# Weights' bound from TensorE products instead of a VectorE reduction, no filling products, and three more units with one exponential

## The chip, the cores and the metric

The kernel runs on one core of a Trainium2 chip. The metric is device microseconds of one execution, taken as the median of several runs. A profiled execution has its own time; its trace covers a span that is a little shorter. The engines are named as the profile names them: PE (TensorE's products) with PEld (its weight loads), DVE (VectorE), ACT (ScalarE), POOL (GpSimd) and SP (SyncE, which issues the DMAs).

## The reference

Linear attention with positive random features is followed by a two-layer network. Batch, heads, sequence and head width are 8, 8, 576 and 64, there are 128 features, and the network has widths 512, 2048 and 512 over 8 x 576 = 4608 tokens.

```python
scale = 1.0 / np.sqrt(np.sqrt(D))
q_s, k_s = (q * scale, k * scale)

def phi(x):
    proj = np.einsum('bhsd,md->bhsm', x, omega)
    sq = np.sum(x * x, axis=-1, keepdims=True) / 2.0
    h = proj - sq
    h = h - np.max(h, axis=-1, keepdims=True)
    return np.exp(h) / np.sqrt(m)
q_p, k_p = (phi(q_s), phi(k_s))
kv = np.einsum('bhsm,bhsd->bhmd', k_p, v)
z = np.sum(k_p, axis=2)
num = np.einsum('bhsm,bhmd->bhsd', q_p, kv)
den = np.einsum('bhsm,bhm->bhs', q_p, z)[..., None] + 1e-06
attn = (num / den).astype(np.float32)
...
h = x @ w_in          # x: attn, heads side by side, 4608 x 512
g = 0.5 * h * (1.0 + erf(h * inv_sqrt2))
return (g @ w_out).astype(np.float32)
```

The two weight matrices come in as 64-bit floats and are brought to 32 bits on the core.

## The kernel before, in words

**Units.** A unit is one batch entry with two heads; there are 32, numbered in order of the batch, so units 0 to 3 are the first batch entry. Units 0 to 7 are "plain": for each, `pair` (L657) and `shared` (L664) make the projections of k and q in 18 tiles of 128 x 128, which lie in five groups in the accumulation memory (PSUM); `top` (L669, DVE) takes the row maxima of a group. Then there are two ways to the exponential. In mode 0, `exp_tiles` (L673, ACT) takes each of the 18 tiles with its own maximum as the bias. In mode 1, `shift_tiles` (L678, DVE) subtracts the maxima group by group, five instructions in all, and `exps` (L682, ACT) then takes all 2304 columns in one instruction. `X['m0']` says how many units are of mode 0. After that come `kv` (L689), a copy of its result (L697, L698), the transposes of q (`q_trans` L727, copied out by `q_copy` L731), the numerator and denominator (`num_plain` L737), the reciprocals (`rcp`, L763 to L766) and the division (`div`, L800). Units 8 to 31 use products of split halves (L902, L924, L1003, L746).

**Weights.** Each matrix comes in eight pieces of 128 partitions x 1024 numbers (1 MB each as 64-bit words), first `w_in` and then `w_out`. `w_load` (L422) brings a piece into one of two buffers `raw`. On it work `w_hi` (L426, ACT; the upper words to a float), `w_rmax` (L438, DVE; the largest absolute upper word of each partition), `w_lo` (L435, ACT; the lower words), `w_shift` (L442, DVE; three bits to the left) and `w_round` (L453, POOL; adds the lower part), which leaves the 32-bit piece in `w32`. When all eight pieces of a matrix have their maximum, `wchain_a` to `wchain_f` (L500, L503, L506, L509, L512, L518 to L521) make one power of two of it for the whole core, the scale. With it `w_high` (L485, ACT) and `w_low` (L489, DVE) split the matrix into a high and a low half of 16 bits.

**Network.** The 4608 tokens are cut into blocks of 128, eleven times 384, and 256. Block 0 is computed in 32 bits straight from `w32` (L1176 first layer, L1187 gelu, L1202 second layer), so it needs no scale. All later blocks use three products of halves for each 32-bit product (L1181 first layer, L1205 to L1207 second layer).

**Order.** A planner goes through all operations with a cost for each, their due times (tables `STARTS`, `UDUE`, `OFF`) and a hand-kept list of operations that come first (`FIRST`). Its result is the fixed order of instructions on each engine; on the chip, each engine takes its instructions in that order and waits where an input is not there. While the planner's clock lies between 5 and `X['wk']` = 100 us and PE has nothing ready, it puts in a `fill` (L381): four products of the identity, whose result nobody reads.

**Accumulation memory.** There are eight banks: two fixed ones (`hb`), three of a ring `at` and three of a ring `acc`. The plain units of the first batch entry may take any of them, the others `at` alone.

Of the kernel before, what the change touches and what calls it, by code (L numbers as in the profile page):

```python
# [11 lines left out]
BF16 = mybir.dt.bfloat16  # L12
# [7 lines left out]
P = 128  # L20
T = 384
# [6 lines left out]
X = dict(fb=793.51, fbp=-272.45, fb0=327.13, fbb=-89.81, fbw=0.0, pm=0.088, tsw=1.28, wmaxp=0, plain=8, kvp=8, eb0=8, ttr=1,  # L28
         pair=0, amax=0, qm=1, xm=0, km=0, prelu=1, vs=1, rm=1, wk=100.0, wk0=5.0, nd=1, sr=0, pmx=0, m0=5)
# [3 lines left out]
STARTS = (526.64, 413.1, 498.14, -519.29, 750.73, 290.96, 409.8, 1471.02, 410.3, 561.38, 1804.53, 1092.9, 2449.47, 1437.07)  # L33
UDUE = (138.05, 1052.37, 451.76, -315.56, -8.29, -412.87, -648.85, -667.31, -702.59, -616.51, 659.91, -322.47, 26.1, 555.78,
# [4 lines left out]
OFF = dict(block_be=26.55, block_high=27.77, block_low=-66.27, block_out=-28.64, block_scales=3.6, block_spread=19.77,  # L39
           bound_b=-1.8, bound_c=-2.45, chain_a=-30.63, chain_b=-10.13, chain_c=-20.24, den=42.52, div=27.82, exp_tiles=19.68,  # L40
           exps=188.48, g_high=-4.72, g_low=-2.69, gelu=-0.61, k_high=-188.65, k_low=1.15, k_shift=6.34, kv=-46.75, kv_a=19.82,
           kv_b=26.2, kv_b2=28.0, kv_c=85.59, kv_d=-177.32, kv_split=-133.22, kvz_plain=-8.08, load_dup=-16.98, load_om=49.87,
           load_two=-48.56, load_v=-10.04, load_vraw=0.87, load_vst=9.94, mm1=-0.7, mm2=6.86, nothing=115.9, num=-9.4,
           num_plain=-14.95, p2=-1.38, pair=14.61, proj=20.5, proj_add=90.32, proj_lo=-1.05, proj_q=-2.91, q_back=-44.1,
           q_blocks=93.79, q_copy=3.3, q_high=-144.85, q_low=-2.94, q_max=87.36, q_max2=100.29, q_max3=-0.43, q_max4=12.08,
           q_max5=4.81, q_max6=-30.09, q_shift=-0.46, q_trans=-45.18, rcp=31.74, shared=-0.95, shift_tiles=7.84,
           split_om=35.99, store=-8.53, store_dma=-54.03, top=-1.35, v_a=53.83, v_b=-6.0, v_max=-0.96, v_scales=80.74,
           w_hi=58.87, w_high=6.68, w_lo=0.74, w_load=-11.85, w_low=3.77, w_rmax=11.16, w_round=-18.28, warm=5.19,
           wchain_a=35.94, wchain_b=91.67, wchain_c=-1.79, wchain_d=18.88, wchain_e=5.29, wchain_f=-87.86, x_high=-1.56,
           x_low=0.31, zeros=71.27)  # L50
FIRST = (1, 3, 0, 2, 6, 7, 8, 40, 4, 5, 42, 110, 76, 144, 41, 142, 10, 9, 151, 157, 44, 13, 43, 11, 14, 15, 47, 74, 16, 45, 17,
# [208 lines left out]
def favor_attention_ffn(ctx: ExitStack, tc: tile.TileContext, qT, kT, v, omT, w_in, w_out, out):  # L260
# [281 lines left out]
    def weights_in(win, i):  # L542
# [19 lines left out]
        if X['rm']:  # L562
            return
# [833 lines left out]
```

## Time and profile before

| what | value |
|---|---|
| median of 3 runs | 976.95 us (976.17 to 978.94) |
| the profiled execution | 975.53 us |
| its span | 973.8 us |
| PE busy | 963.4 us, 6324 instructions |
| DVE busy | 715.4 us, 1948 instructions |
| ACT busy | 730.0 us, 1504 instructions |
| POOL busy | 350.4 us, 560 instructions |

An engine's busy time is the time in which at least one of its instructions is under way. PE's products overlap, so the duration of one (322 ns for L1181) is longer than the time until the next starts; how many products pass in a stretch of the chain of waits gives the pace. Filling products count as busy like all others. Rows of a timeline begin with start and length in us; rows of groups hold busy time, mean ns of one, and what ended the idle time before them.

### The profile page before, as it was taken

How to read it: one execution, taken by the hardware profiler on the slowest of the kernel's cores; microseconds unless marked ns; L12 is line 12 of the kernel's file. 1: busy time of each engine (PE TensorE's matmuls, PEld its weight loads, DVE VectorE, ACT ScalarE, POOL GpSimd, SP SyncE). 2: the span in 40 equal slices, each digit the busy share in tenths (PEclk: the TensorE clock that was granted, in tenths of full speed). 3: DMA queues.
4: the chain of work that ended last, by engine and by line, in shares of the span. 5: the costliest groups of instructions: out<-in, count | busy, mean ns of one | idle time of the engine just before them, and what ended most of it. 6: DMA issues, size and time to landing. Idle time of an engine off the chain costs nothing.

```text
span 973.8 us, 18152 instructions
## 1 busy us (share of the span) xinstructions
PE 963.4 (99%) x6324; PEld 602.3 (62%) x6324; DVE 715.4 (73%) x1948; ACT 730.0 (75%) x1504; POOL 350.4 (36%) x560
## 2 busy tenths in 40 slices
PE   8999999999999999999999999999999999999998
PEld 7777665665566666666565665566656656555576
DVE  5899899977888889878797888777767778621111
ACT  6979897887689879787798878877776986643243
POOL 2444334742166264353255335245216522200000
PEclk9999999999999999999999999999999999999999
DMA  8756123321041041031221132022003200000000
GB/s 305 229 182 227 70 73 134 98 82 55 1 118 61 26 139 47 25 91 45 75 82 49 30 127 66 14 72 61 24 33 86 62 23 12 1 33 1 1 34 22
DMA packets 39083, 70.96 MB, mean 73 GB/s; under 512 B 5712, under 2 KB 14288, under 8 KB 38992
## 3 DMA queue, kind: packets, MB, share of 16 engines
q1 hardware_dynamic: 38992, 69.81, 23.1%
q8 instruction: 50, 0.82, 0.4%
q14 instruction: 41, 0.34, 0.1%
HBM read 60.36 MB, written 9.44 MB: 72 GB/s over the span
## 4 chain that ended last, share of the span: by engine, by line
PE 96%; DVE 2%; DMA 1%; ACT 0%; issue 0%; SPq 0%; ACTq 0%; DVEq 0%
PE hb L1181 37%; PE acc L1205 12%; PE acc L1207 12%; PE acc L1206 12%; PE at L746 4%; PE at L924 3%; PE at L902 3%; PE at L1003 2%; PE hb L381 2%; PE hb L1176 2%; PE acc L1202 1%; PE at L657 1%; PE at L737 1%; PE at L689 1%; PE hb L689 1%; PE at L727 1%
## 5 line engine op out<-in xcount | busy, mean ns | idle before, releaser
L1181 PE MATMUL hb<-xh,wih 128*128 128x384 f16 (+1 forms) x768 | 247.2, 322 | 0.6 <-DVE gl L1197 0.4
L1181 PE MATMUL hb<-xl,wih 128*128 128x384 f16 (+1 forms) x768 | 247.2, 322 | 0.0
L1181 PE MATMUL hb<-xh,wil 128*128 128x384 f16 (+1 forms) x768 | 247.1, 322 | 0.0
L894 POOL TENSOR_TENSOR r<-xt,r 64x256 fp32r<-64x256 f32 (+2 forms) x216 | 171.8, 814 | 202.7 <-ACT r L889 161.3
L1205 PE MATMUL acc<-woh,gh 128*128 128x512 f16 (+1 forms) x560 | 211.4, 377 | 0.0
L1207 PE MATMUL acc<-wol,gh 128*128 128x512 f16 (+1 forms) x560 | 210.5, 376 | 0.0
L1206 PE MATMUL acc<-woh,gl 128*128 128x512 f16 (+1 forms) x560 | 210.5, 376 | 0.0
L1197 DVE SCALAR_TENSOR_TENSOR gl<-hb,bs,gh 128x384 f16<-128x384 f32 (+1 forms) x192 | 115.2, 600 | 126.0 <-ACT gh L1193 124.2
L1181 PEld LDWEIGHTS <-wih 128*128 128x128 f16 x1536 | 147.0, 98 | 95.2 <-issue 1.7
L1189 ACT ACTIVATE hb<-hb,bs 128x384 f32<-128x384 f32 (+1 forms) x192 | 104.5, 545 | 86.8 <-PE hb L1181 84.5
L1193 ACT ACTIVATE gh<-hb,bs 128x384 f16<-128x384 f32 (+1 forms) x192 | 109.2, 569 | 51.5 <-PE acc L1207 35.5
L1181 PEld LDWEIGHTS <-wil 128*128 128x128 f16 x768 | 75.1, 98 | 50.2 <-issue 1.6
L889 ACT CAST r<-xt 128x256 fp32r<-128x256 f32 (+2 forms) x216 | 81.5, 403 | 25.8 <-PE at L902 10.5
L1207 PEld LDWEIGHTS <-gh 128*128 128x128 f16 x576 | 56.4, 98 | 64.5
L1205 PEld LDWEIGHTS <-gh 128*128 128x128 f16 x576 | 56.1, 97 | 47.4 <-issue 0.4
L1206 PEld LDWEIGHTS <-gl 128*128 128x128 f16 x576 | 56.5, 98 | 42.1
L803 DVE TENSOR_TENSOR w<-at,rt 64x128 f32<-64x128 f32 (+6 forms) x168 | 54.7, 325 | 4.3 <-DVE rt L770 0.5
L757 ACT ACTIVATE dt<-at,vsc 64x288 f32<-64x288 f32 x96 | 47.6, 495 | 5.2 <-PE at L746 3.0
L902 PE MATMUL at<-om,r 128*128 128x256 f32 x216 | 50.3, 325 | 0.2
L924 PE MATMUL at<-r,om 128*128 128x288 f32 x192 | 50.4, 351 | 0.0
L906 ACT COPY lo<-at 128x256 f32<-128x256 f32 (+1 forms) x120 | 40.4, 349 | 2.2 <-PE at L902 1.5
L963 DVE TENSOR_TENSOR ql<-qt,qh 128x576 fp32r<-128x576 f32 x48 | 37.3, 782 | 6.1 <-ACT qh L960 6.0
(218 smaller groups left out, 1690.6 us busy)
## 6 DMA issues: line engine op xcount, KB each, us to landing
xt<-in_kT SPq DMA_DIRECT2D x56, 288.0 KB, 3.8
xt<-in_qT SPq DMA_DIRECT2D x56, 288.0 KB, 3.6
out_x<-o SPq DMA_DIRECT2D x35, 256.0 KB, 2.1
raw<-in_w_in SPq DMA_DIRECT2D x16, 512.0 KB, 5.2
raw<-in_w_out SPq DMA_DIRECT2D x16, 512.0 KB, 4.6
w<-in_v SPq DMA_DIRECT2D x6, 1280.0 KB, 6.1
wol<-in_v SPq DMA_DIRECT2D x6, 320.0 KB, 5.9
vt<-in_v SPq DMA_DIRECT2D x2, 320.0 KB, 4.1
```

Of the source, the lines that this page charges most:

```text
L803: nc.vector.tensor_tensor(x[r, c0:c1], ps[r, r0:r1], rt[r, r0:r1], op=ALU.mult)
L889: nc.scalar.copy(G['r', u, x][:, 0:b - a], xf[:, a:b])
L894: nc.gpsimd.tensor_tensor(r, xf[D:, a:b], r, op=ALU.subtract)
L902: nc.tensor.matmul(o[:, t], r[:, t * P:(t + 1) * P], om, start=True, stop=True)
L924: nc.tensor.matmul(G['pp', u, NK + g][:, 0:HS], om[:, i], xr_part(u, NK + g), start=(i == 0), stop=(i == 1))
L1181: nc.tensor.matmul(h[:, 0:t], w, (G['xh', n, j], G['xh', n, j], G['xl', n, j])[k][:, 0:t], start=(i == 0), stop=(i == 3 * NJ - 1))
L1189: nc.scalar.activation(h, h, AF.Gelu, scale=G['bs', n][:, 2:3])
L1193: nc.scalar.activation(G['gh', n, c][:, 0:t], G['h', n, c][:, 0:t], AF.Copy, scale=G['bs', n][:, 3:4])
L1197: nc.vector.scalar_tensor_tensor(G['gl', n, c][:, 0:t], G['h', n, c][:, 0:t], G['bs', n][:, 3:4], G['gh', n, c][:, 0:t], op0=ALU.mult, op1 ...
L1205: nc.tensor.matmul(acc, gh[:, s], woh[:, c, c0:c1], start=(c == 0), stop=False)
L1206: nc.tensor.matmul(acc, gl[:, s], woh[:, c, c0:c1], start=False, stop=False)
L1207: nc.tensor.matmul(acc, gh[:, s], wol[:, c, c0:c1], start=False, stop=(c == NF - 1))
```

## The change

It has three parts, and all the planner's tables are new.

1. `w_rmax` is gone. In its place `w_gram` multiplies, on PE, each of a piece's eight 128 x 128 squares with itself; the operand is the upper 16 bits of each 32-bit number of the finished piece, read as bf16. Four pieces add up in one bank of accumulation memory (`GP = 4`). After the fourth, `w_gmax` (DVE) takes the maximum of the bank's 128 columns. The diagonal holds sums of squares, so its maximum bounds the square of the largest weight; `wchain_e` and `wchain_f` halve the exponent. Since the operand is the finished piece, this stands behind `w_round`, where `w_rmax` stood behind the load.
2. `X['wk']` goes from 100 to 0, so no `fill` is put in. (A flag inside `fill` changes too, without effect since it isn't called.)
3. `X['m0']` goes from 5 to 2: units 2, 3 and 4 take mode 1. `shift_tiles` now writes to the unit's own buffer.

```diff
-X = dict(fb=793.51, fbp=-272.45, ..., vs=1, rm=1, wk=100.0, wk0=5.0, nd=1, sr=0, pmx=0, m0=5)
+X = dict(fb=839.08, fbp=-293.81, ..., vs=1, rm=1, wk=0.0, wk0=5.0, nd=1, sr=0, pmx=0, m0=2, gm=1, rawn=2)
...
-FIRST = (1, 3, 0, 2, 6, 7, 8, 40, 4, 5, 42, 110, 76, 144, 41, 142, 10, 9, 151, 157, 44, 13, 43, 11, 14, 15, 47, 74, 16, 45, 17,
+FIRST = (1, 3, 76, 6, 2, 0, 8, 7, 42, 41, 40, 144, 4, 5, 111, 153, 9, 10, 159, 15, 11, 43, 146, 16, 12, 74, 13, 44, 17, 49, 47,
...
+    def w_gram(pc):
+        o = G['gram', pc.win, pc.i // GP][:, 0:P]
+        for x in range(8):
+            a = pc.b.bitcast(BF16).rearrange("p (x m t) -> p x m t", x=8, t=2)[:, x, :, 1]
+            nc.tensor.matmul(o, a, a, start=(pc.i % GP == 0 and x == 0), stop=(pc.i % GP == GP - 1 and x == 7))
+
+    def w_gmax(win, g):
+        nc.vector.tensor_reduce(wmax[:, win, g:g + 1], G['gram', win, g][:, 0:P], axis=AX.X, op=ALU.max)
...
     def wchain_f(win):
         e, s, r = (wsc[:, win, i:i + 1].bitcast(I32) for i in range(3))
         one = float(1 << 23)
-        if X['rm']:
+        if X['gm']:
+            nc.gpsimd.tensor_scalar(e, e, 0.5, 65 * one, op0=ALU.mult, op1=ALU.add)
+        elif X['rm']:
...
-        if X['rm']:
+        if X['rm'] and not X['gm']:
             op('DVE', 1.23, w_rmax, pc, r=[rk], w=[('wmax', win, i)])
...
+        if X['gm']:
+            g = ('gram', win, i // GP)
+            op('PE', 0.46, w_gram, pc, r=bk, w=[g] if i % GP else [], new=[] if i % GP else [(ANY[:2], g)])
+            if i % GP == GP - 1:
+                op('DVE', 0.25, w_gmax, win, i // GP, r=[g], w=[('wmax', win, i // GP)])
+            return
...
-        nc.vector.tensor_tensor(et[:, ts], pv, G['nm', u][:, ts].unsqueeze(2).broadcast_to([P, n, M]), op=ALU.add)
+        nc.vector.tensor_tensor(u.et[:, ts], pv, G['nm', u][:, ts].unsqueeze(2).broadcast_to([P, n, M]), op=ALU.add)
```

In the rows below, `w_71` is `w32` (which also holds the second exponential buffer and the intermediate results of every second unit), `hb_84` and `hb_85` are the two fixed banks, and `om_66` is the 32-bit features. Line numbers of the changed kernel are about 30 higher: L438 is `w_hi` there, L447 `w_lo`, L463 `w_shift`, L474 `w_round`, L456 `w_gram`, L459 `w_gmax`, L701 `top`, L710 `shift_tiles`, L714 `exps`, L721 `kv`, L769 `num_plain`, L832 `div`, L1208 block 0's first layer.

DVE before, where the eighth piece is prepared and the chain to the first scale begins:

```order
L438 TENSOR_REDUCE wmax<-raw 128x1
L800 TENSOR_TENSOR xa<-hb_84,rt 128x128
L800 TENSOR_TENSOR xa<-hb_84,rt 128x160
L500 TENSOR_REDUCE wcm<-wmax 128x1
L697 COPY kvz<-at 128x2x64
L698 COPY kvz<-at 128x2x64
L442 TENSOR_SCALAR w_71<-w_71 128x1024
```

DVE now, where the ninth piece is prepared and the same chain begins:

```order
L832 TENSOR_TENSOR xa<-acc,rt 128x224
L832 TENSOR_TENSOR xs<-acc,rt 128x64
L463 TENSOR_SCALAR w_71<-w_71 128x1024
L459 TENSOR_REDUCE wmax<-at 128x1
L519 TENSOR_REDUCE wcm<-wmax 128x1
L701 TENSOR_REDUCE nm<-at 128x4
```

The chain's first step moved from ahead of the eighth shift to behind the ninth one; all fifteen `shift_tiles` of units 2 to 4 stand ahead of that place.

ACT before, around the third and fourth piece of `w_in`, with the single tiles of units 2 and 3:

```order
L673 ACTIVATE et<-at,nm 128x128 x4
L426 ACTIVATE w_71<-raw 128x1024
L673 ACTIVATE w_71<-acc,nm 128x128 x8
L731 COPY w_71<-at 128x512
L435 ACTIVATE w_71<-raw 128x1024
L673 ACTIVATE w_71<-acc,nm 128x128 x2
```

ACT now, around the same two pieces:

```order
L438 ACTIVATE w_71<-raw 128x1024
L447 ACTIVATE w_71<-raw 128x1024
L714 ACTIVATE et<-et 128x2304
L438 ACTIVATE w_71<-raw 128x1024
L447 ACTIVATE w_71<-raw 128x1024
L714 ACTIVATE w_71<-w_71 128x2304
```

The tiles of units 2 and 3 that stood between the conversions have become one row for each unit.

PE before, from the fifth unit's `kv` on; a line with dots stands for the repeated pairs of a fill:

```order
L689 MATMUL at<-vt_73,et 128x65 x8
L689 MATMUL at<-vt_73,et 128x130
L727 MATMUL at<-ident,et 128x128 x4
L381 LDWEIGHTS ident
L381 MATMUL hb_84<-ident 128x128
...
L727 MATMUL at<-ident,et 128x128 x4
```

PE now, up to and behind the same `kv`; the dots stand for the sixth and seventh pieces' repeated pairs:

```order
L769 MATMUL hb_84<-w_71 64x288 x2
L769 MATMUL hb_85<-w_71 64x288 x2
L456 LDWEIGHTS w_71
L456 MATMUL at<-w_71 128x128
...
L721 MATMUL at<-vt_73,et 128x65 x8
L721 MATMUL at<-vt_73,et 128x130
L759 MATMUL at<-ident,et 128x128 x4
L769 MATMUL acc<-w_71 64x288 x4
L1208 MATMUL hb_84<-xa,w_71 128x128 x4
```

The fills are gone, and sixteen products of the sixth and seventh pieces stand ahead of the fifth unit's `kv`, which PE can't take before them.

More of the change, by code (lines that the diff above doesn't have):

```diff
@@ L26 @@
 TBS = (128,) + (384,) * 11 + (256,)
[L28 to L34, printed above, removed]
[4 rows of a table removed]
@@ L39 @@
[L39 to L50, printed above, removed]
@@ L51 @@
-FIRST = (1, 3, 0, 2, 6, 7, 8, 40, 4, 5, 42, 110, 76, 144, 41, 142, 10, 9, 151, 157, 44, 13, 43, 11, 14, 15, 47, 74, 16, 45, 17,
[31 rows of a table removed]
+X = dict(fb=839.08, fbp=-293.81, fb0=263.31, fbb=-376.95, fbw=0.0, pm=0.04, tsw=1.28, wmaxp=0, plain=8, kvp=8, eb0=8, ttr=1,
+         pair=0, amax=0, qm=1, xm=0, km=0, prelu=1, vs=1, rm=1, wk=0.0, wk0=5.0, nd=1, sr=0, pmx=0, m0=2, gm=1, rawn=2)
+STARTS = (779.85, 585.97, 916.67, -314.13, 1045.31, 698.63, 521.82, 1618.1, 567.54, 886.13, 1800.89, 1492.52, 2869.69, 1677.7)
@@ new lines @@
+UDUE = (347.21, 1019.61, 554.69, -499.66, 7.6, -468.66, -761.12, -633.4, -489.83, -769.64, 361.02, -64.35, -133.36, 200.62,
[4 rows of a table added]
+OFF = dict(block_be=3.95, block_low=47.0, block_out=35.7, block_scales=57.56, bound_a=50.36, bound_b=-10.62, bound_c=17.88,
+           chain_a=11.77, chain_b=68.87, chain_c=0.23, chain_d=11.02, den=-1.6, div=-4.76, exp_tiles=-6.87, exps=59.86,
+           g_high=-39.33, g_low=3.5, gelu=-8.53, identity=-0.8, k_low=59.48, k_shift=-31.72, kv=-14.64, kv_a=-83.1,
+           kv_b=-14.21, kv_b2=0.08, kv_c=-4.21, kv_d=28.76, kv_split=3.12, kvz_plain=29.33, load_dup=27.05, load_two=6.05,
+           load_v=-21.7, load_vraw=-0.49, load_vst=-86.44, mm1=0.19, mm2=7.04, nothing=0.19, num=-49.21, num_plain=-0.35,
+           p2=-25.63, proj=0.12, proj_add=-147.92, proj_lo=17.36, proj_q=-4.64, q_back=23.65, q_blocks=82.74, q_copy=-0.37,
+           q_high=-4.28, q_low=1.97, q_max=-109.1, q_max2=-39.07, q_max3=-89.65, q_max4=1.05, q_max5=55.91, q_max6=-21.03,
+           q_shift=-73.36, q_trans=70.28, rcp=2.98, shared=26.32, shift_tiles=-21.2, store=-3.35, store_dma=0.86, top=-14.03,
+           v_a=0.43, v_b=2.06, v_copy=-45.85, v_max=56.68, v_scales=4.49, v_spread=-19.77, w_gmax=57.53, w_gram=0.66,
+           w_hi=-39.84, w_high=31.62, w_lo=-6.44, w_load=-79.15, w_low=-14.14, w_round=52.33, w_shift=-24.52, warm=-15.81,
+           wchain_a=-14.94, wchain_c=3.3, wchain_e=-11.25, wchain_f=28.75, x_high=-36.0, x_low=-33.99, zeros=-17.28)
@@ L272, in favor_attention_ffn @@
     NF = F // P
+    GP = 4
     R2 = 2 * S
@@ L325, in favor_attention_ffn @@
     bufs = dict(at=3, h=2, acc=3, nm=2, cm=2, ct=2, cg=2, zr=2, km=2, kvz=1, qh=1, kvz2=1, qh2=1, dt=1, rt=1, rc=2, mx=1, nq=1, mc=1, kvs=1,
-                vsc=2, bs=4, be=2, xs=4, raw=2, r=2 if X['xm'] else 3, lo=2, qt=2, ql=2 if X['qm'] else 4, kvh=1, kvl=1, xh=8, xl=8, g=3, gh=3, gl=3, o=2)
+                vsc=2, bs=4, be=2, xs=4, raw=X['rawn'], r=2 if X['xm'] else 3, lo=2, qt=2, ql=2 if X['qm'] else 4, kvh=1, kvl=1, xh=8, xl=8, g=3, gh=3, gl=3, o=2)
     for k, b in bufs.items():
@@ L380, in fill @@
         for i in range(4):
-            nc.tensor.matmul(hb[0][:, T:], iz[:, 0:P], iz[:, P:], start=True, stop=True)
+            nc.tensor.matmul(hb[0][:, T:], iz[:, 0:P], iz[:, P:], start=False, stop=True, skip_group_check=True)
     def load_om():
@@ L496, in wchain_a @@
     def wchain_a(win):
+        if X['gm']:
+            nc.vector.tensor_reduce(wcm[:, win:win + 1], wmax[:, win, 0:NF // 2 // GP], axis=AX.X, op=ALU.max)
+            return
         w = [i for i in range(NF // 2) if i % 2 == 0 or not X['pmx'] >> (i // 2 + 4 * (1 - win)) & 1]
@@ L511, in wchain_e @@
     def wchain_e(win):
-        nc.vector.tensor_scalar(wsc[:, win, 0:1].bitcast(I32), G['wps', win][:, P:P + 1].bitcast(I32), 0x7ff00000 if X['rm'] else 0x7f800000, None, op0=ALU.bitwise_and)
+        nc.vector.tensor_scalar(wsc[:, win, 0:1].bitcast(I32), G['wps', win][:, P:P + 1].bitcast(I32), 0x7f000000 if X['gm'] else 0x7ff00000 if X['rm'] else 0x7f800000, None, op0=ALU.bitwise_and)
     def wchain_f(win):
@@ L561, in weights_in @@
             op('DVE', 1.21, w_sign, pc, r=[rk], w=bk)
+        if X['gm']:
+            g = ('gram', win, i // GP)
+            op('PE', 0.46, w_gram, pc, r=bk, w=[g] if i % GP else [], new=[] if i % GP else [(ANY[:2], g)])
+            if i % GP == GP - 1:
+                op('DVE', 0.25, w_gmax, win, i // GP, r=[g], w=[('wmax', win, i // GP)])
+            return
         if X['rm']:
```

82 rows, old and new, of tables (FIRST, UDUE) are left out of this document.

## The prediction

> **What bounds the kernel now.** I read the page's summary first, then the engines' busy time by stage, then the chain of waits by stage. The page:
>
> ```profile
> span 973.8 us, 18152 instructions
> PE 963.4 (99%) x6324; PEld 602.3 (62%) x6324; DVE 715.4 (73%) x1948; ACT 730.0 (75%) x1504; POOL 350.4 (36%) x560
> PEclk9999999999999999999999999999999999999999
> PE 96%; DVE 2%; DMA 1%; ACT 0%; issue 0%; SPq 0%; ACTq 0%; DVEq 0%
> ```
>
> PE is the chain, at full clock throughout. But busy is not useful: the fills are in it. I cut the span where the pieces of the weights mark it: the first piece's conversion, the ninth shift, and the last shift, which coincides with the first product of block 1.
>
> ```profile
> 17.45 1.17 ACT L426 ACTIVATE w<-raw 128x1024 f32<-128x1024 f32 x1 [0.44 <-DMA raw<-in_w_in]
> 67.26 0.67 DVE L442 TENSOR_SCALAR w<-w 128x1024 int32<-128x1024 int32 x1
> 111.91 0.33 PE L1181 MATMUL hb<-xh,wih 128*128 128x384 f16 x1
> 111.97 0.68 DVE L442 TENSOR_SCALAR w<-w 128x1024 int32<-128x1024 int32 x1
> ```
>
> Busy time in these stretches (length; PE, PEld, DVE, ACT, POOL; clock; DMA share; GB/s):
>
> ```profile
> 0.00:17.40 17.40, 14.39 (x162) 12.05 (x164) 5.95 (x19) 7.80 (x25) 2.13 (x8) 1.00 0.85 289
> 17.40:67.30 49.90, 47.62 (x546) 38.93 (x547) 43.17 (x108) 44.56 (x108) 22.72 (x16) 1.00 0.76 241
> 67.30:112.00 44.70, 44.34 (x353) 33.41 (x352) 41.08 (x80) 38.72 (x59) 19.29 (x19) 1.00 0.48 164
> 112.00:850.00 738.00, 737.24 (x4519) 444.62 (x4518) 603.04 (x1705) 595.77 (x1231) 306.21 (x517) 1.00 0.20 60
> ```
>
> The chain of waits in the second, the third and the last of them, by line:
>
> ```profile
> by line: PE hb L381 25.0%; PE hb L689 8.8%; PE at L657 8.8%; PE acc L737 7.8%; PE hb L737 7.7%; PE acc L657 6.6%; PE at L727 5.8%; PE acc L689 4.1%; PE at L689 4.1%; PE acc L727 3.5%; DVE rc L764 2.5%; PE at L737 2.2%; PE hb L1176 1.3%; PE
> by line: PE hb L1176 32.3%; PE acc L1202 26.1%; PE at L737 10.0%; PE at L689 9.0%; PE hb L381 7.4%; PE at L657 7.3%; PE at L727 4.7%; PE at L664 2.6%; ACT g L1187 0.6%; issue 0.1%
> by line: PE hb L1181 42.1%; PE acc L1205 13.6%; PE acc L1207 13.5%; PE acc L1206 13.4%; PE at L746 4.3%; PE at L924 3.0%; PE at L902 2.9%; PE at L1003 2.5%; PE at L737 0.5%; DVE w L803 0.4%; PE acc L1202 0.3%; DVE xl L1170 0.3%; PE at L657
> ```
>
> So stage A (17.4 to 67.3) holds 25.0% x 49.9 = 12.5 us of fills, PE time with nothing to do; with the reciprocal's 1.2 us PE has some 14 us to spare. DVE idles 6.7 us and ACT 5.3 us there: these two, in turns, hold the stage. Stage B (67.3 to 112) has 7.4% x 44.7 = 3.3 us of fills, and the rest is PE's own work: PE holds it. Behind 112 there is no spare PE time to speak of (737.24 of 738.0) and no fill; all that can be won there is already won. A gain or loss is made ahead of 112 us and carried to the end unchanged.
>
> **The change part by part.** The rows of the operations:
>
> ```profile
> L381 PE MATMUL hb<-ident 128*128 128x128 bf16 x312 | 21.8, 219 | 2.0 <-DVE w L698 0.6 <-DVE nm L669 0.5 <-ACT g L1187 0.4
> L438 DVE TENSOR_REDUCE wmax<-raw 128x1 f32<-128x1024 f32 x16 | 19.3, 1207 | 1.0 <-DMA raw<-in_w_in 1.0
> L678 DVE TENSOR_TENSOR et<-at,nm 128x512 f32<-128x512 f32 (+1 forms) x13 | 7.6, 613 | 0.0
> 47.56 2.23 ACT L673 ACTIVATE et<-at,nm 128x128 f32<-128x128 f32 x8
> L682 ACT ACTIVATE et<-et x16: 2122/2124/2129, 81.6 to 826.3; 128x2304 f32<-128x2304 f32 x16
> L453 POOL TENSOR_TENSOR w<-w x12: 2348/2370/2377, 19.8 to 88.7; 128x1024 int32<-128x1024 int32 x12
> 9.83 0.58 PE acc L664 x8
> 10.41 3.01 PE hb L381 x52
> 13.42 0.58 PE acc L664 x8
> 72.18 1.98 PE hb L1176 x16
> 22.69 0.27 DVE L715 TENSOR_REDUCE km<-kvz 128x2 f32<-128x128 f32 x1
> 62.98 2.37 POOL L453 TENSOR_TENSOR w<-w 128x1024 int32<-128x1024 int32 x1 [3.81 <-ACT qh L731]
> ```
>
> and, of the reduction L438 alone, DVE's busy time up to and behind the ninth shift:
>
> ```profile
> 0.00:67.30 67.30, 9.62 (x8) 1.00 0.78 253
> 67.30:112.00 44.70, 9.68 (x8) 1.00 0.48 164
> ```
>
> *The reduction goes.* 16 x 1.207 = 19.3 us of DVE, eight in each stage: -9.7 us in A, -9.7 in B.
>
> *Three units in mode 1.* On DVE 15 `shift_tiles` x 0.613 = +9.2 us; by the order all stand ahead of the ninth shift, so in A. On ACT 54 tiles at 2.23 / 8 = 0.279 us, 15.1 us, become 3 x 2.12 = 6.4: -8.7 us, in A too. A unit's exponential now waits for its last group's shift; that costs at worst one group's maximum and shift (two instructions of about L678's 0.6 us) and the 2.1 us of the whole exponential for each of three units, 10 us, and nothing where another unit's work fills the time, as units 2 and 3 are interleaved. I take nothing, since fifteen shifts and the other units' work stand between.
>
> *Gram products.* 52 fills took 3.01 us, 58 ns each, of the same shape and type: 128 x 58 ns = 7.4 us, 3.7 in each stage. The upper end is the pace of 128-column products of 32 bits, 1.98 / 16 = 124 ns: 15.8 us. I take 58 ns, the equal form; the stride of the operand is the one doubt. In A it lies in PE's 14 us to spare; in B it is on the path. `w_gmax`, four reductions of 128 columns like L715's, is 0.27 us each on DVE, 0.5 in a stage.
>
> *Fills go.* Their time is waiting time, which stays: 0 in A; at best a product that came in during a group of four starts up to 0.23 us sooner. In B the 3.3 us are free for Gram: between 0 (the waits stay) and -3.3; I take -3.3, because the work behind is there and the table is new.
>
> *The scale comes later.* It needs the last rounding (2.37 us behind the shift), Gram and a maximum. The first halves' products stand at 111.91, and `w_in`'s last rounding began at 62.98 and ended by 65.4, so some 40 us cover it; gone if roundings slip by tens of us. For `w_out` block 1's first-layer products stand between. Nothing.
>
> *Gram as a wait.* PE takes its queue in order, so behind a Gram that waits for POOL stand num, kv and block 0. In A the spare 14 us cover 1.7 us at each of eight places. I take nothing, with the other end as a rival.
>
> *The new tables* move nearly everything, DMAs too, but the pieces still need two buffers each freed by `w_lo`; DMA has 0.76 and 0.48 of its time in use in A and B, so I give it nothing.
>
> Sum. Stage A: DVE's work is the same (-9.7 + 9.2 + 0.5), ACT's is 8.7 us less. If DVE, now without ACT's turns, never idled, A would be 6.7 us shorter; PE's own 36 us and 3.7 of Gram fit into 43. If it idles as before, 0. I take half, -3.4. Stage B: DVE -9.2 is off the path; PE -3.3 + 3.7 = +0.4. Behind 112: 0, with 1 us either way for the order. Total -3.0 us: span 973.8 to 970.8, the profiled execution 975.53 to 972.5. The median of the runs lies 1.4 us above that execution; from it, 976.95 - 3.0 = 974.0 us. That is just what a measurement of this kernel can tell from no change (0.3%, 2.9 us).
>
> **The rivals.**
>
> *DVE fills up (more gain).* A -6.7, and in B half of Gram hides as well, -1.3: 976.95 - 8.0 = 969.0. For it: no other engine is needed more than 45 us in A. Against: DVE idled 6.7 us though it had always work of four units.
>
> *It evens out (no change).* A gains 0 to 1 because the whole-unit exponentials and PE's in-order waits put DVE to idling anew, B pays Gram: 977.
>
> *PE stands at Gram (slower).* In B there are 3.3 us of spare PE time for eight places, 0.4 each. If at each PE comes before the rounding ends and stands for half of its 2.37 us, that is 9.5 us, less 3.3; with 1 us won in A and nothing else, 976.95 - 1 + 6.2 = 982. It decides once the mean stand in B is over 0.8 us. For it: `w_rmax` had nothing behind it on PE, and POOL is the last of four engines a piece goes through. Against: POOL is busy under half of the time, and the order puts some 2 to 8 us of other products between the Grams of B (counted in it, at the chain's paces).
>
> *The clock drops without fills (slower).* With the fills, PE's longest time without real products is between L664's two rows, from 10.41 to 13.42 us; without, PE idles there. If a third of PE's 36 us in A ran at half clock, 12 us are added, of which half hides in what it waits for anyway; with Gram in B and no gain in A, 976.95 + 6 + 0.4 = 983.4. Against it in this trace: PE sat idle for 2.0 us and the clock of the first stretch is still 1.00.
>
> ```profile
> 8.66 0.37 PE L657 MATMUL at<-om,xt 64*128 64x128 f32 x1 [1.96 <-DMA xt<-in_kT]
> ```
>
> [...]
>
> **How the numbers follow.** Chances: the sum above 0.40 (971.5 to 976.5 about 974.0), more gain 0.15, no change 0.25, Gram 0.13, clock 0.07. Of the first, half lies beyond the bound of 0.3%, which is 974.0: faster 0.15 + 0.20 + a little = 0.38; same 0.20 + 0.22 = 0.42; slower 0.20. The range takes in the larger gain and most of the Gram rival: 968 to 981.
>
> **What the changed profile would show.** Right: the ninth shift at about 64 us and the last at about 108; the chain in A with DVE, ACT and idle PE where the fills stood; 128 Gram products at 58 ns; no waits over 0.4 us at Gram in B; clock 1.00. Wrong: PE standing at Gram for POOL's rounding; the ninth shift at 67 or later; a Gram product at 100 ns or more; a clock under 1.00 ahead of 112 us; or a different amount of PE waiting behind it.

## The result and the profile after

| kernel | device us, median (lowest to highest, runs) | ratio to the kernel before, 95% interval | mean granted clock of the runs |
|---|---|---|---|
| before | 976.98 (975.85 to 978.94, 6) | | 1.00 (the profiled one) |
| changed | 983.35 (981.10 to 988.29, 6) | 1.0065 (1.0048 to 1.0082) | 0.988 to 0.996 |

The change costs 6.4 us where -3.0 was forecast. The profiled execution took 984.35 us, 1.0 above the median. Its page, the span, PE's busy time, the clock by slices and the chain by engine:

```profile
span 982.4 us, 17675 instructions
PE 961.7 (98%) x6140; PEld 594.4 (61%) x6140; DVE 714.0 (73%) x1951; ACT 719.6 (73%) x1453; POOL 351.6 (36%) x560
PEclk9999999999999999999999999999999999999999
PE 80%; DVE 10%; ACT 5%; issue 2%; DMA 1%; POOL 1%; SPq 0%; ACTq 0%; POOLq 0%; DVEq 0%
```

PE held 96% of the chain, now 80%; the sixteen per cent went mostly to DVE, ACT and issue. The row of clocks looks unchanged, but a slice is 24.6 us long and a digit 9 means 0.9 or more. The stages, cut at the same times as before (length; PE, PEld, DVE, ACT, POOL; clock; DMA share; GB/s), the ninth and the last shift, and block 1's first product:

```profile
0.00:17.40 17.40, 12.79 (x109) 10.36 (x110) 6.31 (x21) 8.34 (x25) 2.30 (x9) 0.90 0.90 299
17.40:67.30 49.90, 41.54 (x366) 29.95 (x366) 44.84 (x103) 31.24 (x49) 20.08 (x16) 0.93 0.65 211
67.30:112.00 44.70, 43.66 (x357) 32.12 (x357) 36.79 (x79) 41.52 (x67) 25.20 (x21) 1.00 0.59 193
112.00:850.00 738.00, 735.71 (x4519) 444.22 (x4518) 597.88 (x1695) 589.63 (x1219) 301.35 (x503) 1.00 0.21 60
70.85 0.68 DVE L463 TENSOR_SCALAR w<-w 128x1024 int32<-128x1024 int32 x1
108.80 0.68 DVE L463 TENSOR_SCALAR w<-w 128x1024 int32<-128x1024 int32 x1
121.44 0.34 PE L1213 MATMUL hb<-xh,wih 128*128 128x384 f16 x1
```

The clock was 0.90 and 0.93 in the first two stages. The ninth shift came at 70.85 us, 3.6 later than before; the last one at 108.80, 3.2 earlier. But the last shift no longer marks the end of the head: block 1's first product came at 121.44 us, where before it stood beside that shift at 111.91 (in the new order more of the other products stand ahead of it, too). The chain of waits in stage A and in stage B, by line:

```profile
by line: DVE nm L701 15.8%; DVE rc L796 11.7%; DVE w L463 11.6%; DVE rt L798 6.8%; DVE et L710 6.5%; PE at L689 6.2%; DVE rt L795 6.2%; DVE xa L832 5.8%; PE hb L769 4.6%; DVE w L710 4.4%; issue 4.2%; PE hb L721 3.5%; DVE rc L797 3.2%; PE ac
by line: PE hb L1208 28.9%; PE acc L1234 23.7%; PE at L769 10.0%; PE acc L456 7.9%; PE at L689 7.3%; PE at L721 4.5%; PE at L759 3.4%; PE at L696 2.6%; DVE w L463 1.3%; ACT qh L763 1.3%; DVE rt L798 1.1%; issue 0.9%; DVE rt L795 0.9%; DVE x
```

Stage A is DVE's chain now. One row stands out: `rc` L796, the addition of 1e-6 to nine denominators in each partition, is 11.7% of 49.9 us, 5.8 us. Compare its group, and that of the shift, before (L764, L442) and now (L796, L463):

```profile
L442 DVE TENSOR_SCALAR w<-w 128x1024 int32<-128x1024 int32 x16 | 10.8, 677 | 0.0
L764 DVE TENSOR_SCALAR rc<-rt 128x9 f32<-128x9 f32 x16 | 5.3, 329 | 0.6
L463 DVE TENSOR_SCALAR w<-w 128x1024 int32<-128x1024 int32 x16 | 13.3, 833 | 0.0
L796 DVE TENSOR_SCALAR rc<-rt 128x9 f32<-128x9 f32 x16 | 8.8, 550 | 0.6
```

The same instructions of the same shape became longer. Where, the timeline shows: three of DVE's long ones, each shown below the POOL rounding that ran at that time.

```profile
21.27 2.35 POOL L474 TENSOR_TENSOR w<-w 128x1024 int32<-128x1024 int32 x1 [1.31 <-ACT w L447]
21.44 2.73 DVE L463 TENSOR_SCALAR w<-w 128x1024 int32<-128x1024 int32 x1
33.07 2.36 POOL L474 TENSOR_TENSOR w<-w 128x1024 int32<-128x1024 int32 x1 [1.40 <-DVE w L463]
33.95 1.52 DVE L796 TENSOR_SCALAR rc<-rt 128x9 f32<-128x9 f32 x1
39.18 2.37 POOL L474 TENSOR_TENSOR w<-w 128x1024 int32<-128x1024 int32 x1 [3.75 <-DVE w L463]
40.06 1.52 DVE L796 TENSOR_SCALAR rc<-rt 128x9 f32<-128x9 f32 x1
```

The two additions end at 35.47 and 41.58 us; the roundings that began before them end at 35.43 and 41.55. By these rows DVE stands still until POOL is done, and its row counts that as busy: ahead of 125 us all five long additions of this trace, and the three of the trace before, began beside a rounding and ended 0.03 to 0.04 us behind it; the long shift, whose usual time is 0.68 us, ended 0.55 us behind. Row maxima (L701) and `shift_tiles` (L710) of 512 columns that began beside roundings kept their usual 0.68 us (0.67 to 0.70). Summed over DVE's instructions ahead of 125 us, what each took beyond the usual time of its kind is 2.1 us before and 9.3 us now.

The clock was 0.50 from 10.71 to 14.12 us and from 44.84 to 51.66 us. These times lie on a grid of 3.41 us; in windows on it:

```profile
7.29:10.71 3.42, 0.63 (x6) 0.40 (x8) 1.02 (x2) 2.77 (x10) 0.72 (x1) 1.00 1.01 365
10.71:14.12 3.41, 3.41 (x30) 2.86 (x30) 1.27 (x3) 0.90 (x4) 0.00 (x0) 0.50 1.08 369
41.42:44.84 3.42, 1.67 (x15) 1.25 (x15) 3.18 (x12) 2.28 (x4) 0.79 (x2) 1.00 0.59 199
44.84:48.25 3.41, 3.01 (x18) 2.31 (x20) 2.30 (x8) 3.41 (x6) 1.70 (x2) 0.50 0.02 5
48.25:51.66 3.41, 3.41 (x20) 1.72 (x18) 2.01 (x4) 0.48 (x1) 0.87 (x1) 0.50 0.17 28
```

Behind a window in which PE was busy for 0.63 us, and behind one with 1.67 us, PE ran at half clock: 10.2 us in all, where the kernel before had none.

### The profile page after: what moved, and what is told of

The parts are those of the page before. It is cut to its first block, busy times and chain, and to the rows that moved or that the text cites. A ratio compares the mean times of both kernels' runs of the same rounds, so it can differ in the third digit from the quotient of the medians.

```text
span 982.4 us, 17675 instructions
## 1 busy us (share of the span) xinstructions
PE 961.7 (98%) x6140; PEld 594.4 (61%) x6140; DVE 714.0 (73%) x1951; ACT 719.6 (73%) x1453; POOL 351.6 (36%) x560
## 4 chain that ended last, share of the span: by engine, by line
PE 80%; DVE 10%; ACT 5%; issue 2%; DMA 1%; POOL 1%; SPq 0%; ACTq 0%; POOLq 0%; DVEq 0%
PE hb L1213 32%; PE acc L1237 10%; PE acc L1238 10%; PE acc L1239 10%; PE at L778 3%; PE at L934 2%; PE at L956 2%; PE at L1035 2%; PE acc L1234 1%; PE hb L1208 1%; PE at L689 1%; PE at L769 1%; DVE gl L1229 1%; ACT dt L789 1%; DVE nm L701 1%
## 5 line engine op out<-in xcount | busy, mean ns | idle before, releaser
L926 POOL TENSOR_TENSOR r<-xt,r 64x256 fp32r<-64x256 f32 (+2 forms) x216 | 168.4, 800 | 227.7 <-ACT r L921 151.5
L956 PE MATMUL at<-r,om 128*128 128x288 f32 x192 | 48.2, 344 | 0.2 <-DVE nm L944 0.2
L1035 PE MATMUL at<-vb,w 128*128 128x129 f16 (+3 forms) x432 | 41.0, 212 | 0.2 <-DVE nm L944 0.2
L364 POOL TENSOR_SCALAR w<-et 128x256 f16<-128x256 f32 (+1 forms) x65 | 24.3, 401 | 46.9 <-ACT et L714 37.7
```

Source lines behind the costliest of these rows:

```text
L926: nc.gpsimd.tensor_tensor(r, xf[D:, a:b], r, op=ALU.subtract)
L956: nc.tensor.matmul(G['pp', u, NK + g][:, 0:HS], om[:, i], xr_part(u, NK + g), start=(i == 0), stop=(i == 1))
L1035: nc.tensor.matmul(o[:, hs, 0:w], kk[:, k, t], vb[:, vs, 0:w], start=f and x == 0, stop=end and x == 1, skip_group_check=True)
```

## The experiments

Two theories stood against each other at first: **C**, that the half clock, which the fills had kept away, costs the time, and **O**, that PE waits in those stretches anyway and the loss is DVE's, by **P**, the stand-still beside POOL's rounding. Times are medians (lowest to highest, runs); ratios are to the kernel before on the same chip, whose medians there were 976.8 to 977.7. The experiments ran on four chips, so a difference of one us between two of them is only as good as the intervals of their ratios.

**The fills of the kernel before, thinned.** All left out, or two or one product for each `fill` instead of four:

```diff
     def fill():
-        for i in range(4):
+        for i in range(2):      # or range(1); or nothing at all
             nc.tensor.matmul(hb[0][:, T:], iz[:, 0:P], iz[:, P:], start=True, stop=True)
```

> The kernel before, with its 312 fill products left out and every other instruction in its old place and order. Theory C (the clock: the changed kernel loses 4 to 5 of its 6.4 us because it runs 10.2 us at half clock for want of fills): a granted clock of 0.5 should show ahead of 112 us here too, near 10 us and near any stretch where PE is busy under half of 3.4 us, and the time should be 979 to 983 us. Rival O (the clock drop costs nothing, since PE waits there anyway; the loss is DVE's longer instructions and Gram's 7.2 us): whatever the clock does, 974 to 977 us; the 3.3 us of fills in stage B could give up to -3.

> The kernel before with two products in each fill instead of four, 156 instead of 312 (8.7 us fewer); all else is unchanged. The kernel before without fills ran in 974 to 978 us at a clock of 0.987 to 0.993, and once in 969 at clock 1.00. Theory C with F (each fill product stands in the way of PE's own products at a fair part of its time, some 8 us in all; the fills pay only by keeping the clock): if half of them are enough for the clock, 972 to 974 us at clock 1.00. If they are too few: clock 0.99 and 975 to 978. Rival O (fills cost nothing, as my prediction had it, and neither does the clock): 977 in every case.

> The kernel before with one product in each fill instead of four (78 products, 4.4 us; 13.1 us fewer). With two, 8.7 us fewer, it took 972.4 us at a clock of 0.998 to 1.00; with none, 974 to 978 at 0.987 to 0.993 and once 969.15 at 1.00. If one product is enough for the clock: 970 to 971.5 us. If windows of 3.4 us less than half busy come back (near 10 and 31 us): 972 to 975 with clocks of 0.993 to 0.998, and the runs further apart than with two.

| fill products | us | ratio | clock |
|---|---|---|---|
| 312 (before) | 976.8 to 977.7 | | 0.996 to 1.00 |
| 156 | 972.40 (971.32 to 973.74, 5) | 0.9955 (0.9939 to 0.9971) | 0.998 to 1.00 |
| 78 | 971.34 (970.81 to 974.39, 5) | 0.9943 (0.9921 to 0.9964) | 0.998 to 1.00 |
| 0 | 976.10 (969.15 to 978.45, 10) | 0.9985 (0.9967 to 1.0004) | 0.987 to 0.993; once 1.00 |

By the median alone, leaving all out has no effect, and 976.10 lies in rival O's range. The single runs tell more: nine at a mean clock of 0.990 have a mean of 976.3 us; the one that kept 1.00 took 969.15. So two effects of 7 to 8 us seem to cancel; their size rests on that one run, their direction also on the two rows with fewer fills at full clock. Fills do delay PE's own products, and the lost clock costs about as much. The drop's places without fills:

```profile
10.32:13.73 3.41, 1.33 (x20) 1.06 (x20) 1.38 (x4) 3.01 (x13) 0.00 (x0) 1.00 1.05 383
13.73:27.39 13.66, 13.66 (x79) 12.43 (x76) 7.64 (x15) 9.52 (x23) 4.62 (x5) 0.50 0.84 276
30.80:34.21 3.41, 1.70 (x13) 0.83 (x10) 3.26 (x8) 3.41 (x9) 0.61 (x1) 1.00 0.91 296
34.21:37.63 3.42, 3.41 (x21) 2.32 (x22) 3.32 (x8) 3.42 (x12) 1.75 (x1) 0.50 0.85 279
```

One product in each fill is enough to keep the clock, and that kernel beats the one with four and the one with none; against two the intervals overlap. Its fill group, its first two stages and its ninth shift:

```profile
L381 PE MATMUL hb<-ident 128*128 128x128 bf16 x78 | 8.8, 220 | 4.0 <-ACT w L731 1.5 <-DVE xa L800 0.8 <-DVE w L698 0.6
0.00:17.40 17.40, 13.98 (x134) 11.03 (x134) 6.69 (x20) 8.43 (x26) 2.85 (x9) 1.00 0.85 293
17.40:67.30 49.90, 43.64 (x422) 32.92 (x420) 46.81 (x117) 44.59 (x111) 25.17 (x21) 1.00 0.76 245
62.90 0.67 DVE L442 TENSOR_SCALAR w<-w 128x1024 int32<-128x1024 int32 x1
```

The ninth shift comes 4.4 us sooner than before, with all of DVE's and ACT's work unchanged: what had held stage A was in good part the fills.

**Fills put back into the changed kernel.** First wherever its plan leaves PE idle between 5 and 100 us, then 106 products at five places chosen from the trace:

```diff
+            if o.e == 'PE' and 5.0 < t < 100.0:            # first version
+                for _ in range(int((t - free['PE']) / 0.23)):
+                    fill()
+            if o.e == 'PE' and key_of(o) in FILLS:          # second version
+                fill(FILLS[key_of(o)])
             put(o)
```

> The changed kernel, with fills (groups of four 128-column products, as before had) put where its plan leaves PE idle between 5 and 100 us; the order of all else is kept. Theory C: clock 1.00 throughout and 978 to 980 us. Rival O: clock 1.00 or not, 983 us as the changed kernel; slower, 984 to 986, if the fills stand in the way of PE's own products.

> The changed kernel with 106 fill products (5.9 us at 56 ns) put only at the five places where its trace shows PE standing for 0.8 to 2.8 us in a 3.4 us window that is less than half busy or nearly so: 40 ahead of unit 1's first feature products, 10 ahead of unit 2's second, 28 and 14 ahead of unit 0's num_plain, 14 ahead of unit 4's first. All else is unchanged. Theory C (the half clock costs PE its time wherever it falls, since PE has little to spare: 10.2 us at half cost some 4 us): clock 1.00 in nearly every run, 979 to 980 us, and the runs lie close together. Rival O (PE waits there anyway, so the clock costs nothing; the whole loss is DVE's longer instructions): clock 1.00 and 983 us or above. If fills delay PE's own products: over 984.

The first took 986.52 us (985.35 to 991.20, 4), ratio 1.0105 (1.0076 to 1.0134): 9.9 us of fills, and still two half-clock windows in the profiled execution (granted clock 0.996). They stand behind windows at 28.2 and 55.5 us with PE busy for 1.1 and 1.2 us, so the plan's idle time did not cover all places where PE idles. The second took 981.82 (980.88 to 982.87, 4), ratio 1.0049 (1.0030 to 1.0067), at clocks of 0.998 and 0.999. That is 1.5 below the changed kernel (the intervals of the ratios overlap), not the 3.4 to 4.4 that theory C gave: I had priced 5.9 us of fill products at nothing once more.

**The stand-still taken away.** From the DVE's side, by leaving out the addition of 1e-6 in the first eight units (the denominators then lack it); from POOL's side, with all work kept, by four short roundings instead of a long one. Rival **W** holds that only the work of the addition, or luck with the clock, is behind a gain:

```diff
-            nc.vector.tensor_scalar(rc, rv[:, :, 0], EPS, None, op0=ALU.add)
-            nc.vector.reciprocal(rc, rc)
+            nc.vector.reciprocal(rc, rv[:, :, 0])
...
-        nc.gpsimd.tensor_tensor(pc.b, pc.b, pc.l or raw(pc)[1], op=ALU.add)
+        for x in range(4):
+            nc.gpsimd.tensor_tensor(pc.b[:, x * n:(x + 1) * n], pc.b[:, x * n:(x + 1) * n], lo[:, x * n:(x + 1) * n], op=ALU.add)
```

> The changed kernel without the addition of 1e-6 to the denominator in the first eight units (left out of the computation): the DVE instruction of 0.17 us that took up to 1.5 us beside POOL's rounding is gone, in eight places. Theory P (DVE's instructions that stand still beside POOL's rounding cost 5 to 6 us of DVE's chain in 20 to 65 us, and with it 3 to 5 us of the whole): 978 to 980 us, ninth shift at 65 to 67 us instead of 70.85. Theory C: 982 to 983.5 us, since the clock still falls. If the reciprocal that follows takes over the stand-still, nothing changes (983).

> The same instruction left out of the kernel before (1e-6 in the denominator of the first eight units left out of the computation). There only one of them was long (1.24 us instead of 0.17, on the chain of waits of stage A with 2.5%). Theory P: -1 us, 975.5 to 976.5 us, a small gain since it happens once. Theory C and O: the same, 976 to 977. It shows what the edit is worth where the stand-still hardly occurs.

> The changed kernel with each rounding on POOL (one instruction of 2.35 us) cut into four of 256 columns, some 0.6 us each; all is computed, and the order is kept. Theory P (DVE's shift and its addition in the denominator stand still until POOL's rounding ends, up to 1.5 and 2.7 us at a time): the stand-stills shrink to at most 0.6 us, their sum ahead of 125 us from 9.3 to about 3, and the time from 983.35 to 978 to 980 us. Rival W (leaving the addition out helped only because it is less work on DVE, 0.17 us eight times, and moved the clock's windows by luck): 983 us, or more by POOL's extra instructions.

> The same cut of the rounding in the kernel before with one product in each fill (971.34 us), where the stand-stills ahead of 125 us sum to 2.7 us. Theory P: a smaller gain than in the changed kernel, 0.5 to 1.5 us, 970 to 971 us. Rival W: the same time or a little more, 971 to 972.

| kernel | us | ratio | clock |
|---|---|---|---|
| changed, no addition | 977.59 (975.97 to 983.02, 10) | 1.0016 (0.9995 to 1.0036) | 0.996 to 0.998; three at 0.989 |
| before, no addition | 976.19 (974.95 to 977.68, 10) | 0.9991 (0.9979 to 1.0002) | 0.998 to 1.00 |
| changed, rounding in four | 979.81 (977.74 to 984.79, 8) | 1.0036 (1.0016 to 1.0055) | 0.989 to 1.00 |
| before with one product in each fill, rounding in four | 971.77 (971.52 to 974.14, 4) | 0.9951 (0.9932 to 0.9970) | 0.998 to 1.00 |

In the changed kernel an addition of 0.17 us, done sixteen times, is worth 5.8 us, more than theory P gave, and four short roundings 3.5 us, within its range (by the ratios 4.8 and 2.8). The ninth shift came at 63.53 and 65.07 us instead of 70.85. In the kernel before, the addition is worth 0.9, within the interval of no change, which tells none of the theories apart, and the short roundings nothing, which is W's range there; but there they took nothing away: the stand-stills ahead of 125 us, 2.7 us without the cut, were no less with it (2.9). In the changed kernel with short roundings the groups read:

```profile
L477 POOL TENSOR_TENSOR w<-w 128x256 int32<-128x256 int32 x48 | 34.9, 758 | 19.9 <-ACT w L447 15.1 <-DVE w L463 4.8
L463 DVE TENSOR_SCALAR w<-w 128x1024 int32<-128x1024 int32 x16 | 11.6, 728 | 2.4 <-ACT w L438 2.4
L799 DVE TENSOR_SCALAR rc<-rt 128x9 f32<-128x9 f32 x16 | 4.9, 305 | 0.6
```

POOL has more to do in all (0.758 x 4 = 3.0 us for a piece instead of 2.41), and yet DVE's shift falls from 833 to 728 ns and the addition from 550 to 305; the stand-stills ahead of 125 us sum to 3.2 us instead of 9.3 (without the addition to 1.2). So what DVE loses goes by the length of POOL's instruction, and rival W, which gave 983 us or more here, falls (the intervals of the two ratios just overlap, 1.0016 to 1.0055 and 1.0048 to 1.0082; that the stand-stills shrank with all work kept decides it). About one us of each gain is the clock's (its mean over the runs is 0.9938 in the changed kernel, 0.9948 and 0.9954 here). The three runs at 0.989 took 982.2 to 983.0 us, the seven others 976.0 to 977.9: the same kernel, 5.6 us apart, and the clock is all that the record shows to differ.

So the clock has a price, and theory C stands beside P. The mean clock differs by 0.0083 between those groups, 8.1 us of PE's time, for 5.6 us of the whole: 0.7 for each us lost. In the kernel without fills it is 7.2 us for 0.0097, 9.5 us: 0.76. In the changed kernel 0.995 of 982 us is 4.9 us lost, so 3.4 to 3.7 of its 6.4 us by these prices. Its own six runs, from 981.10 at 0.996 to 988.29 at 0.988, agree (a straight line through them gives 0.8); the eight runs with short roundings give 0.5.

**Fills, no addition, and a quarter of Gram.** The same five places filled, the addition left out, and then only 2 of 8 squares in `w_gram` (the bound then covers a quarter of the weights):

```diff
-        for x in range(8):
+        for x in (0, 7):
             a = pc.b.bitcast(BF16).rearrange("p (x m t) -> p x m t", x=8, t=2)[:, x, :, 1]
```

> The same fills and in addition the addition of 1e-6 to the denominator left out in the first eight units (left out of the computation), so that DVE has no instruction of 0.17 us that grows to 1.5 beside POOL's rounding. Theories C and P together (two independent losses, 4 and 4 to 5 us): 974.5 to 976 us, clock 1.00, no runs at 982 as three of ten had with the addition alone left out (those at clock 0.989). If the gain of leaving the addition out was the clock's only (DVE earlier, so no half-clock stretch behind 40 us): as a_clk, 979 to 980.

> As the kernel with fills and without the addition, and only 2 of the 8 Gram products of each piece (the bound of the weights is then taken over a quarter of them, which leaves out part of the computation): 96 products of 56 ns fewer, 5.4 us of PE. Theory G (Gram's products cost PE their full time where PE is the bound, in stage B: half of them, 2.7 us, in stage A next to nothing): 2 to 3 us below its neighbour. If all of Gram is paid for: 5.4 us below. If it hides in waits: the same time.

With fills and without the addition: 979.24 us (977.56 to 981.75, 10), ratio 1.0021 (1.0009 to 1.0033), no better than without fills, and above the 974.5 to 976 of theories C and P together. Three runs at 0.999 and 1.00 took 977.6 to 977.9, seven at 0.998 took 979.0 to 981.8: five places did not suffice. In the profiled execution the window at 27.8 us, with PE busy for 1.1 of 3.41, was still followed by half clock (0.998 over the whole). With a quarter of Gram 975.64 (974.76 to 977.39, 10), ratio 0.9977 (0.9961 to 0.9994). At clocks of 0.999 and above it is 975.1 against 977.6, so 96 products of 56 ns, 5.4 us, cost 2.5 us; by the medians of all runs, 3.6. For all 128 products that makes 3.3 to 4.8 us.

**DVE relieved, order kept.** The kernel before with one product in each fill, whose reductions read a quarter of the columns (the rest is left out of the bound):

```diff
-        nc.vector.tensor_reduce(..., raw(pc)[2].bitcast(F32), axis=AX.X, op=ALU.max, apply_absolute_value=True)
+        nc.vector.tensor_reduce(..., raw(pc)[2].bitcast(F32)[:, 0:256], axis=AX.X, op=ALU.max, apply_absolute_value=True)
```

> The kernel before with one product in each fill, whose reductions take the maximum of a quarter of the columns (the rest is left out of the bound): about 0.35 us instead of 1.21, 14 us less for DVE, 7 of it ahead of the ninth shift, with everything else in its place. My prediction's step (DVE and ACT hold the first stage in turns; half of what DVE is relieved of comes back): 3 to 3.5 us, 968 us. Rival (in a fixed order DVE's relief is taken up by waits for ACT, POOL and DMA, or ends in stand-stills beside POOL): 970.5 to 972.

969.98 us (969.79 to 970.55, 4), ratio 0.9928 (0.9913 to 0.9944), 1.4 below its neighbour (1.5 by the ratios, whose intervals overlap). The reductions took 405 ns each instead of 1207, so 12.8 us of DVE's work are worth about 1.4 us, not 3 to 3.5, and at most a little more than the rival gave.

**Each part alone in the old order, and the old tables behind the new head.** These three misled me. In the first two, on the kernel before with two products in each fill, the order by hand is carried over operation by operation; Gram stands behind its rounding, or the shifts of units 2 to 4 at the places of their tiles. In the third, the changed kernel (no addition) takes the old tables for what stands behind the written order:

```diff
-X = dict(fb=793.51, ..., m0=5)
+X = dict(fb=793.51, ..., m0=5, gm=1, rawn=2)      # Gram alone; or m0=2, gm=0: units 2 to 4 alone
...
-STARTS = (779.85, ...; UDUE = (347.21, ...; OFF = dict(block_be=3.95, ...     # third: the new tables
+STARTS = (526.64, ...; UDUE = (138.05, ...; OFF = dict(block_be=26.55, ...    # the old ones
```

> One part alone, on the kernel before with two products in each fill (972.4 us): the reductions are replaced by Gram's products, each put directly behind its rounding in the old order, and w_gmax behind the fourth and eighth; units 2 to 4 stay in mode 0, tables and fills stay as they were. DVE has 19.3 - 1.1 = 18 us less to do, PE 7.2 us more. Theory G (PE pays Gram in stage B, about 0.5 to 0.67 us for each us of it, and DVE does not hold the end): 975 to 977 us. Rival D (DVE's relief in stage A is worth more than Gram costs): 968 to 971. If PE stands long for POOL's rounding: 978 and more, with waits at Gram over 4 us in all.

> The other part alone, on the same base (972.4 us): units 2, 3 and 4 take their shift on DVE (15 instructions of 0.61 us, 9.2 us) and one exponential each (ACT 8.7 us less), in the places of the old tiles; reductions stay. DVE then has about 52 us to do in the 50 us of stage A. Theory D (DVE holds stage A): +5 to +9 us, 977 to 981, and the ninth shift 5 to 9 us later. Rival (ACT holds it as much, the two even out): 971 to 974.

> The changed kernel without the addition of 1e-6 (left out of the computation in the first eight units), and behind the written-out order, from about 115 us on, with the tables (start times, due times, offsets, bonuses) of the kernel before; the head is instruction for instruction as in its neighbour, which took 977.6 us (976 to 978 at clock 0.997, 982 to 983 at 0.989). Theory L (the new tables' order behind 115 us loses some 3 us in small PE waits): 973.5 to 975 us at a clock of 0.997. Rival (the late waits follow from the head's lateness, not from the order): 976 to 978.

They took 991.61 us (991.00 to 993.27, 4), ratio 1.0145 (1.0124 to 1.0166); 1005.10 (1004.01 to 1006.83, 4), ratio 1.0282 (1.0260 to 1.0304); and 981.92 (980.14 to 985.73, 10), ratio 1.0047 (1.0034 to 1.0060). None is where a theory put it: the first is above the 978 of "PE stands long", but PE's waits at Gram were 2.6 us there and not over 4. In the first two the last shift came at 123.5 and 120.6 us (107.9 in their base): the old order with other operations in it brings the pieces late. The second also lost some 10 us far behind that: from 480 to 630 us PE was busy for 139.9 us (149.8 in the base), at a clock of 0.95 (1.00). The parts can't be read off these runs; each set of operations has its own order. The third refutes that the new tables are the worse ones behind 115 us: the old ones cost 3 to 4 us more there.

## Why the prediction was wrong

- **"Fills go: 0 in A" failed.** Its reason, that their time is waiting time which stays, is refuted: 13.1 us of fills fewer gave 5.6 us (ratio 0.9943), all 17.5 us fewer 7.9 us in the one run at full clock. That is a bit under half of their time. The row was there: 25.0% of stage A's chain was L381. I read a place on the chain as spare time. This term alone speaks for a gain, and a larger one than forecast.
- **The clock rival happened**, at 0.07 of the chance. Its 983.4 us agree with the 983.35 measured by accident: it assumed 12 us added, half of them hidden; it was 10.2 us at half clock, 5.1 us lost, 3.4 to 3.7 of them paid. What kept its chance small was one pause of 2.0 us at full clock; that the idling without fills would do as little was my estimate, which no run had shown. The length of a pause was the wrong measure: between 41.42 and 44.84 us PE was busy for 1.67 us with no pause over 1.1 us, and the clock fell to 0.50. Nor did one busy window always bring the clock back: without fills PE was busy for all of 13.66 us from 13.73 us on, at a clock of 0.50.
- **A term was missing**: DVE's instructions that stand still beside POOL's rounding, 9.3 us instead of 2.1. Cutting the rounding gave back 3.5 us of the whole with the clock's part in it, leaving out the addition 5.8. I summed DVE's work by durations from before as if they stayed. The prediction's own row for stage A had `rc` L764 with 2.5% of the chain, 1.2 us for one instruction of 0.17. The additions ended with POOL's instruction to 0.04 us; why DVE stands still there no run shows.
- **Stage A's -3.4 failed.** "If DVE never idled" is no measure of what its relief is worth: 12.8 us less of DVE were worth about 1.4 us over both stages. Nor did DVE and ACT alone hold the stage before: with fewer fills and all of their work the ninth shift came 4.4 us sooner. The chain in A went to DVE, but with longer instructions.
- **Gram was right in size**: 24 products at 34.64 us took 1.55 us, which holds the last one's full 0.22 us; they start 57 to 58 ns apart. The cost of 3.3 to 4.8 us stands beside 3.7 in B and 0 in A; how it divides between the stages no run shows. PE stood little for it, 1.2 us once in A and 0.8 once in B (over the 0.4 that the prediction allowed, far from the 0.8 at each of eight places that its rival needed), so that rival is out:

```profile
34.64 1.55 PE L456 MATMUL acc<-w 128*128 128x128 bf16 x24
62.92 0.63 PE L456 MATMUL at<-w 128*128 128x128 bf16 x8 [1.21 <-POOL w L474]
69.48 0.63 PE L456 MATMUL at<-w 128*128 128x128 bf16 x8 [0.77 <-POOL w L474]
PE at L456 <- POOL w L474: 2.0, 2, 1.2
```

- **Behind 112, "0 with 1 us either way" failed.** By an estimate, good to about one us, that takes each product at the pace that it has without gaps, PE had done 5.2 us less of the kernel's own work than before at 115 us, and the span is 8.6 us longer: some 3.4 us are lost later. Of these, 1.9 us show as idle time of PE (6.7 us from 115 us on, before 4.7), in small waits that the kernel before didn't have. The longest totals of PE's waits from 115 us on, before (first row) and now:

```profile
PE hb L1181 <- DVE gl L1197: 0.4, 1, 0.4
PE hb L1213 <- DVE gl L1229: 0.9, 2, 0.5
PE at L934 <- DVE nm L944: 0.6, 2, 0.4
```

The cause of the loss stays open. It isn't the tables alone, as the old ones did worse, and the kernel before without fills, in the unchanged order, also has a wait of 1.7 us there.

- The signs named: the last shift at about 108 us came (108.80), but it proved a poor sign, since block 1's first product came 9.5 us later than before; the ninth was late (70.85 instead of 64); the first scale's chain cost PE one wait of 0.3 us. The clock ahead of 112 us and PE's waiting behind it were the wrong signs that came true. (In the working, the rival with more gain has -1.3 for B, where -3.3 and half of 3.7 make -1.45; nothing hangs on it.)

Forecast were -3.0 us. In a ledger from the runs, fills -8, clock +3.5, stand-stills +2.5 to +5, Gram +3.3 to 4.8, the late loss +3.4 and DVE's relief about -1.4 make +3.3 to +7.3; 6.4 were measured. These terms were measured in different kernels and act on each other (PE, too, waits for DVE, 1.05 us for L832 up to 45.24 us), so their sum is a rough ledger and not a proof; what the three units' move to DVE costs by itself is in none of them.

## What to carry to other kernels

Filler products in front of an engine's own work can cost a good part of their time (here a bit under half) even where the plan shows idle time; use as few as keep the clock (here 78 in place of 312 kept it at 0.998 to 1.00), and find the number by the granted clock of every run and not by the median, since a saving and a loss of equal size can hide in it. When work moves between engines, an instruction's old duration need not hold (here the addition's mean went from 329 to 550 ns, with its long ones beside POOL's roundings): look at the longest of a group beside its shortest before taking the mean. A written-out order is worth something only with the operations it was made for, so a part of such a change can't be priced by putting it alone into the old order.

## What the runs showed of the hardware

- Half clock (0.50) stood behind windows of 3.41 us in which PE was busy for 0.63 and 1.67 us (changed kernel), 1.33 and 1.70 us (before without fills) and 1.54 us (changed, no addition); in the one of 1.67 us no pause was over 1.1 us. Behind one of 1.72 us in the changed kernel the clock stayed 1.00, and so it did behind the emptiest of the kernel before between 4.48 us and PE's last product, 2.22 us.
- Half clock lasted 3.41 us behind the window of 0.63 us, 6.82 behind that of 1.67 and 13.66 behind that of 1.33, with PE busy for 3.41, 6.42 and 13.66 us of them. So one busy window doesn't always end it; what does, these runs don't show.
- It began at 10.71 and 44.84 us in the changed kernel, ten times 3.41 us apart, and at 13.73 and 34.21 us in the kernel before without fills, six times 3.41 apart; 10.71 and 13.73 are 3.02 apart, so the windows lie differently in the two traces. Whether that puts the runs of one kernel into groups, as 976 to 978 and 982 to 983 us without the addition, is not shown, since each kernel has one trace.
- A DVE addition over 9 columns, 0.17 us, took up to 1.52 us beside POOL's rounding of 2.36 us, and a shift of 0.68 us 2.73; with POOL's instruction cut into four the longest addition took 0.68 us, and the shift's mean was 728 ns instead of 833.
